# Thirty small marker transfers on SyncE's DMA queue of a decode kernel, behind w3 and behind w4

## The chip, the cores and the metric

The kernel runs on one core of one Trainium2 chip. The metric is the device time of one execution in microseconds, lower is better. A core has TensorE (PE), VectorE (DVE), ScalarE (ACT), GpSimd (POOL) and SyncE (SP). Sixteen DMA engines move data between the chip's memory (HBM) and the core's SBUF; here SP issues nearly all transfers, and ACT two small ones.

## The reference: what is computed

One decode step of a parallel block for 4 sequences, one token each, with D = 576, in bf16:

```python
xn = layernorm(x)                                   # x: 4 x 576
q  = (xn @ wq) as 32 heads of 128                   # wq: 576 x 4096
k, v = the last 2048 of 8192 cached rows            # 4 x 16 kv heads x 2048 x 128, two q heads each
o  = softmax(q k^T / sqrt(128)) v
a  = o @ wo                                         # wo: 4096 x 576
h  = gelu(layernorm(xn) @ w1); hs = shifted(h) @ w2 # 576 x 576 each
x1 = xn + hs
b  = x1 + gelu(layernorm(x1) @ w3) @ w4             # w3: 576 x 4608, w4: 4608 x 576
out = x + a + b
```

The caches dominate: 4 x 16 x 2048 x 128 values of 2 bytes are 33.6 MB for K, and as much for V. With the weights 88.5 MB are read.

## The kernel before

**The stages.** First come the small matmuls with w1, w2, wq and w3, in the order in which these weights land. Then come 16 chunks of K (2 MB each, four ring slots in `kring`): PE transposes each in 8 blocks (line 485), DVE and ACT copy the blocks out of PSUM into `ktb` (469 and 468), and PE multiplies them with q (492). Softmax follows for all heads together. Then come 8 chunks of V (4 MB each, four slots in `vring` and `kring`): DVE spreads the probabilities into padded tiles (545), and PE multiplies (553). Last come h2 @ w4 (36 row blocks) and o @ wo (32 row blocks in five parts of 13, 10, 5, 3 and 1), all added up in one PSUM bank by the helper at line 392, after which DVE and ACT write the halves of the output.

**The order of the work.** The program is collected in one list for each engine. `add` takes a function, the events to wait for, the event that it signals, and a key; line 613 sorts each list by key, and `emit_program` (632) writes the waits and then the instruction. A list is executed in order, so a wait holds all that is behind it on its engine. `add_dma` (192 to 203) puts a transfer into SP's list unless told otherwise; its `dma_start` is line 199, and when the transfer has landed it has added 16 to the semaphore named by its key.

**SP's list around the change.** The keys of w1, w2, wq and w3 are -50, -49, -48 and -47 (lines 269 to 272), and none of them waits. The 16 K chunks have keys 0 to 15 (286 to 288): chunks 0 and 1 wait for nothing, chunks 2 and 3 for q, and each later one for the transposes of the chunk that had its slot. The V chunks have keys KS + 0 to KS + 7, with KS = 132 (289 to 292); the last is cut in two. w4 has key KS + 8 = 140 (273) and waits for a PV step that frees its place; it takes the place of V chunks in `vring`. The five parts of wo have keys 148 to 152 (295 to 299); their waits are for PV steps no later than that of w4. The output is the only other transfer behind them; ACT issues it, as it does x at the start.

**Layouts.** Every transfer on SP's queue has 128 partitions as its outer dimension on the SBUF side. A K chunk is 128 rows of 16 KB, w3 and w4 are 128 rows of 41,472 B, and the last part of wo is 128 rows of 1152 B. The transfers x in and the output have 4 rows of 1152 B.

**POOL's list** holds the memsets and masks of the start, with keys from -100 to below -82, and no waits on DMAs.

Of the kernel before, what the change touches and what calls it, by code (L numbers as in the profile page):

```python
# [6 lines left out]
BF16 = mybir.dt.bfloat16  # L7
# [30 lines left out]
def bass_parallel_sum__sliding_block_cached__mixer_s_mlp__decode_kernel(  # L38
# [24 lines left out]
    NCV, NTV = len(VCH), 2 * NT  # L63
# [6 lines left out]
    with ExitStack() as ctx:  # L70
        def sb(name, shape, dt):
            return ctx.enter_context(nc.sbuf_tensor(name, shape, dt))

        def sem(name):
            return ctx.enter_context(nc.semaphore(name))
# [95 lines left out]
        S = {}  # L171
# [12 lines left out]
        dma_count = {}  # L184
# [3 lines left out]
        def add(engine, emit, waits=(), sig=None, key=0.0, inc=None):  # L188
            seqc[0] += 1
            prog[engine].append(Op(emit, waits, sig, key, seqc[0], inc))  # L190

        def add_dma(pairs, skey, waits=(), key=0.0, engine="sp"):
            if skey not in S:
                S[skey] = sem("s_" + "_".join(str(k) for k in (skey if isinstance(skey, tuple) else (skey,))))
            dma_count[skey] = dma_count.get(skey, 0) + 16 * len(pairs)

            def emit(e):
                for o_, i_ in pairs:
                    e.dma_start(o_, i_).then_inc(S[skey], 16)  # L199
            add(engine, emit, waits, None, key)  # L200
            return ("dma", skey, dma_count[skey])
# [19 lines left out]
        KS = float(NB + 4)  # L221
# [4 lines left out]
        P = lambda *a, **k: add("pool", *a, **k)  # L226
# [52 lines left out]
        def v_src(c, t0, t1):  # L279
# [2 lines left out]
            return A_v_cache[2 * bp:2 * bp + 2, :, k0:k0 + 4 * NTV, :].rearrange(  # L282
                "b h (i t) d -> (b h) i (t d)", t=NTV)[:, :, Dh * t0:Dh * t1]

        t_done = lambda c: f"T{NBLK * c + NBLK - 1}"
        for c in range(NC):
            w = [t_done(c - N_CB)] if c >= N_CB else (["q"] if c >= 2 else [])
# [6 lines left out]
        ev_wo, WOR, a = [], [], 0  # L294
# [176 lines left out]
        for n in range(NB):  # L471
            c, k = n // NBLK, n % NBLK
# [178 lines left out]
        e = nc.tensor  # L651
        emit_program("pe", "pe", e)
        with nc.Fori(0, N_LOOP, engines=[PE]) as it:
# [7 lines left out]
            for j in range(LB):  # L661
                emit_T(e, j, wait)
                if j % NBLK == 2:
                    k = (j // NBLK - 1) % N_CB
# [53 lines left out]
```

## Time and profile before

| what | value |
|---|---|
| median of 2 runs | 214.18 us (213.99 to 214.36) |
| the profiled execution's own time | 213.93 us |
| its span, first to last instruction | 212.6 us |
| mean granted TensorE clock | 0.928 |
| busy: PE, PEld, DVE, ACT, POOL | 172.5, 133.7, 111.9, 58.6, 15.6 us |
| read from HBM | 88.49 MB, 416 GB/s over the span |

A line of a stage or a group names the line of the program, the engine, the operation and "out<-in", with a count behind an x. "Busy" is the time in which an engine executes. The DMA share is the time that the DMA engines' packets took, as a share of 16 engines: 1.0 means that all of them are busy throughout. A packet is one piece that one engine moves. The queues are numbered: q1 is SP's, q10 ACT's, q8 and q14 carry instructions and tables. A row of issues gives the time from an issue to the moment at which the whole transfer has landed, on the last of its engines.

### The profile page before, as it was taken

The page shows a single profiled execution, that of the slowest core. Times are in us where ns is not written, and L with a number is a line of the kernel's source. Part 1 is how long each engine was busy: PE and PEld are TensorE (multiplying, and loading weights), DVE is VectorE, ACT ScalarE, POOL GpSimd, SP SyncE. Part 2 cuts the span into 40 slices and gives each one's busy share as a digit, 9 for nine tenths or more (in the row PEclk, how much of TensorE's full clock was granted, in tenths as well). Part 3 has the DMA queues.
Part 4 walks back from the last instruction along what each step waited for, and adds up shares of the span by engine and source line. Part 5 has one row for each costly group of instructions (what it writes and reads, how often), then busy time and mean ns, then how long its engine had stood idle before and what let it go on. Part 6 is the DMA issues. An engine that isn't in the chain of part 4 may idle for free.

```text
span 212.6 us, 4856 instructions
## 1 busy us (share of the span) xinstructions
PE 172.5 (81%) x2212; PEld 133.7 (63%) x2216; DVE 111.9 (53%) x168; ACT 58.6 (28%) x69; POOL 15.6 (7%) x38
## 2 busy tenths in 40 slices
PE   1456147999999999999996089999989598997495
PEld 0222014888878888887774048988868487883262
DVE  5433200477776777777764869995575444003000
ACT  2004001366665566666656520000000000000000
POOL 8991000000000000000000000000000000000000
PEclk9997855899999999999999589999999889999799
DMA  6999999999999999999999999999999999999993
GB/s 242 453 444 445 429 396 416 432 425 427 429 416 438 432 422 429 435 422 424 432 444 438 444 407 459 413 425 453 407 444 438 419 425 410 451 476 393 407 408 131
DMA packets 5066, 88.65 MB, mean 417 GB/s; under 512 B 568, under 2 KB 704, under 8 KB 1216
## 3 DMA queue, kind: packets, MB, share of 16 engines
q1 hardware_dynamic: 5040, 88.49, 97.7%
q8 instruction: 8, 0.13, 0.3%
q14 instruction: 2, 0.02, 0.0%
q10 hardware_dynamic: 16, 0.01, 0.0%
HBM read 88.49 MB, written 0.00 MB: 416 GB/s over the span
## 4 chain that ended last, share of the span: by engine, by line
DMA 47%; PE 45%; DVE 4%; SPq 1%; ACT 1%; issue 1%
PE ps L485 23%; DMA vring<-in_A_wo_dram 15%; DMA vring<-in_B_w_dram 13%; DMA vring<-in_A_v_cache_dram 12%; PE ps L553 11%; DMA kring<-in_A_k_cache_dram 7%; PE ps L492 6%; PE ps L430 2%; SPq L199 1%; DVE vring L520 1%; DVE rmax L498 1%; DVE ktb L545 1%; PE ps L514 1%; PE ps L347 1%; ACT ktb L468 0%
## 5 line engine op out<-in xcount | busy, mean ns | idle before, releaser
L469 DVE COPY ktb<-ps 128x1024 bf16<-128x1024 bf16 x80 | 53.8, 689 | 23.5 <-PE ps L485 23.4
L485 PEld LDWEIGHTS ps<-perm_bf,kring 128*128 128x128 bf16 x1024 | 58.2, 98 | 8.3 <-issue 7.6
L485 PE MATMUL ps<-perm_bf,kring 128*128 128x128 bf16 x1024 | 61.7, 220 | 0.2
L468 ACT ACTIVATE ktb<-ps 128x1024 bf16<-128x1024 bf16 x48 | 48.0, 1023 | 32.5 <-PE ps L485 32.1
L545 DVE TENSOR_TENSOR ktb<-kring,mH_bf 128x4096 bf16<-128x4096 bf16 x16 | 36.2, 2286 | 14.6 <-PE ps L553 14.6
L553 PE MATMUL ps<-vring,ktb 128*128 128x256 bf16 x256 | 30.3, 282 | 4.3 <-DMA vring<-in_A_v_cache_dram 3.5
L553 PEld LDWEIGHTS ps<-vring,ktb 128*128 128x128 bf16 x256 | 25.7, 101 | 8.5 <-issue 3.6
L553 PE MATMUL ps<-kring,ktb 128*128 128x256 bf16 x256 | 28.6, 273 | 0.9 <-DMA kring<-in_A_v_cache_dram 0.9
L553 PEld LDWEIGHTS ps<-kring,ktb 128*128 128x128 bf16 x256 | 25.0, 98 | 4.5 <-issue 1.1
L608 ACT ACTIVATE out_sb<-ps 4x288 bf16<-4x288 f32 x1 | 0.4, 399 | 84.6 <-PE ps L392 84.6
L492 PE MATMUL ps<-ktb,Qs 128*32 128x512 bf16 x272 | 17.8, 382 | 1.2 <-ACT ktb L468 1.2
L430 PE MATMUL ps<-vring,xs 128*8 128x320 bf16 (+1 forms) x72 | 4.5, 429 | 7.6 <-DMA vring<-in_B_w_dram 7.6
L492 PEld LDWEIGHTS ps<-ktb,Qs 128*32 128x32 bf16 x272 | 5.7, 96 | 6.7 <-DVE ktb L469 1.4
L514 PE MATMUL ps<-vring,pick_bf 128*32 128x256 bf16 x64 | 3.9, 411 | 6.4 <-DVE rinv L532 6.4
L609 DVE CAST out_sb<-ps 4x288 bf16<-4x288 f32 x1 | 0.4, 449 | 15.7 <-PE ps L392 15.7
L392 PE MATMUL ps<-vring,h2T_sb 128*4 128x288 bf16 x72 | 6.2, 347 | 3.1 <-DMA vring<-in_B_w_dram 3.1
L571 DVE TENSOR_SCALAR tmp<-ps,maskd 128x128 f32<-128x128 f32 x2 | 0.7, 350 | 14.8 <-PE ps L553 14.8
L430 PEld LDWEIGHTS ps<-vring,xs 128*8 128x8 bf16 x72 | 2.1, 110 | 9.8 <-DMA vring<-in_B_w_dram 8.0
L330 PE MATMUL ps<-ident_bf,xp_bf 4*128 4x4 bf16 x15 | 0.8, 163 | 8.1 <-DVE xp_bf L314 5.0
L392 PEld LDWEIGHTS ps<-vring,h2T_sb 128*4 128x4 bf16 x72 | 3.7, 101 | 5.8 <-DMA vring<-in_B_w_dram 3.6
L514 PEld LDWEIGHTS ps<-vring,pick_bf 128*32 128x32 bf16 x64 | 2.0, 118 | 8.2 <-DVE rinv L532 6.9
L239 POOL MEMSET ktb<- 128x8192 bf16 x1 | 6.9, 6924 | 0.0
(93 smaller groups left out, 78.6 us busy)
## 6 DMA issues: line engine op xcount, KB each, us to landing
kring<-in_A_k_cache_dram SPq DMA_DIRECT2D x16, 2048.0 KB, 13.8
vring<-in_A_v_cache_dram SPq DMA_DIRECT2D x4, 4096.0 KB, 24.6
kring<-in_A_v_cache_dram SPq DMA_DIRECT2D x3, 4096.0 KB, 34.0
vring<-in_B_w_dram SPq DMA_DIRECT2D x2, 5184.0 KB, 25.1
kring<-in_A_wq_dram SPq DMA_DIRECT2D x1, 4608.0 KB, 15.7
kring<-in_A_v_cache_dram SPq DMA_DIRECT2D x2, 2048.0 KB, 27.4
vring<-in_A_wo_dram SPq DMA_DIRECT2D x1, 1872.0 KB, 26.9
vring<-in_A_wo_dram SPq DMA_DIRECT2D x1, 1440.0 KB, 29.8
```

Of the source, the lines that this page charges most:

```text
L199: e.dma_start(o_, i_).then_inc(S[skey], 16)
L239: P(lambda e: e.memset(ktb[:, NKT // 2 * 1024:NKT * 1024], 0.0), key=-92, inc=(("E", LB - 2), 1))
L347: ins = e.matmul(ps[:, w, :], lhsT=zeros_bf[:, 0:128], rhs=zeros_bf[:, :], start=True, stop=True)
L392: return e.matmul(ACC[h], lhsT=lhsT, rhs=rhs, start=start, stop=stop, tile_position=(0, 32 * h), skip_group_check=True)
L430: ins = e.matmul(H2ps[k][32 * j:32 * j + 2 * B].rearrange("b (p t) -> b p t", t=n), lhsT=x_at(2, s_), rhs=w[:, :, 9 * j + t0:9 * j + t0 + ...
L468: return "act", lambda e: e.activation(out=ktbuf[:, n % NKT], in_=tb[n % 4], func=ACTF.Copy)
L469: return "dve", lambda e: e.tensor_copy(out=ktbuf[:, n % NKT], in_=tb[n % 4])
L485: ins = e.transpose(tb[j % 4][:, t, :], kslot_t(k)[:, 8 * kb + t, :], perm_bf[:])
L492: ins = e.matmul(Sps[32 * u:32 * u + 32, q, :].rearrange("p (t i) -> p t i", t=16), lhsT=Qs[:, k, 32 * u:32 * u + 32], rhs=ktgrp[:, (4 * k ...
L514: ins = e.matmul(ps[32 * j:32 * j + 32, 4 + qt, 256 * ih:256 * (ih + 1)].rearrange("p (t a e) -> p t a e", a=NPAIR, e=2), lhsT=pick_bf[:, ...
L545: return lambda e: e.tensor_tensor(out=PTpad[:, n % 4], in0=PTv[:, qt, NH * h:NH * (h + 1), bp, :].unsqueeze(2).to_broadcast([128, NH, NX, ...
L553: ins = e.matmul(ps[:, 0, 0:256], lhsT=PTpad[:, 2 * (k % 2) + h, 2 * g:2 * g + 2].rearrange("p t h e -> p (t h e)"), rhs=vslot(k)[:, Dh * ...
```

## The change

A new tile, `mark_sb`, of 16 partitions is put behind the others. `marks(n, key)` issues 15 transfers from the top left corner of wo: k rows of 4 + k values, for k from 15 down to 1, so 15 rows of 38 bytes first and one row of 10 bytes last. Each has columns of its own in the tile, and all of a group count on one semaphore. Group 0 has keys of about -45, so it stands between w3 (-47) and K chunk 0 (0). Group 1 has keys just over KS + 8.01, so it stands between w4 (140) and the first part of wo (148). None of the 30 waits for anything. POOL gets two waits, one for each group's full count of 15 x 16 = 240; their key of -1 puts them at the end of its list. Nothing reads `mark_sb`.

```diff
@@ behind v_src, ahead of the loop over the K chunks
+        mark_sb = sb("mark_sb", [16, 2, 256], BF16)
+
+        def marks(n, key):
+            a = 0
+            for k in range(15, 0, -1):
+                add_dma([(mark_sb[0:k, n, a:a + 4 + k], A_wo[0:k, 0:4 + k])], ("mark", n), (), key + 0.001 * (16 - k))
+                a += 4 + k
+        marks(0, -45)
+        marks(1, KS + NCV + 0.01)
+        for n in range(2):
+            P(lambda e, n=n: e.wait_ge(S["mark", n], dma_count["mark", n]), key=-1)
         t_done = lambda c: f"T{NBLK * c + NBLK - 1}"
```

## The prediction, as it was put on record before the result

> **What bounds the kernel now.** I read the page's head and DMA part first, then the chain of waits, then the table of busy time by stage, and last the issues of the DMA queue that the change touches.
>
> ```profile
> span 212.6 us, 4856 instructions
> DMA packets 5066, 88.65 MB, mean 417 GB/s; under 512 B 568, under 2 KB 704, under 8 KB 1216
> q1 hardware_dynamic: 5040, 88.49, 97.7%
> q8 instruction: 8, 0.13, 0.3%
> q10 hardware_dynamic: 16, 0.01, 0.0%
> ```
>
> The reader is to see 97.7%: the packets of SP's queue alone fill all 16 DMA engines for nearly the whole span. The counts also show how a transfer is cut. SP issues 35 transfers of 128 rows, and 35 x (128 + 16) is the 5040 of q1: one packet for each row, and one small one on each of 16 engines that reports the end. The two transfers of 4 rows on ACT's queue, x in and the output, make 16 packets: 4 rows and 4 reports each. The stages (PE, PEld, DVE, ACT, POOL, then granted clock, DMA share, GB/s):
>
> ```profile
> 2.50:29.00 26.50, 9.98 (x84) 4.81 (x84) 10.18 (x34) 3.07 (x7) 13.80 (x31) 0.86 1.01 429
> 92.00:118.00 26.00, 22.83 (x380) 18.27 (x376) 17.56 (x28) 15.61 (x15) 0.00 (x0) 0.99 1.01 433
> 185.00:197.40 12.40, 10.33 (x80) 7.40 (x79) 1.68 (x5) 0.00 (x0) 0.00 (x0) 1.00 1.02 438
> 197.40:208.00 10.60, 8.53 (x112) 5.36 (x114) 0.00 (x0) 0.00 (x0) 0.00 (x0) 0.84 0.95 402
> 208.50:210.40 1.90, 1.26 (x20) 0.53 (x16) 0.00 (x0) 0.00 (x0) 0.00 (x0) 1.00 0.30 116
> ```
>
> The DMA share is 1.0 from 2.5 us to 197.4 us. So the span is the time in which the slowest of 16 engines works through its own list, and a packet put anywhere into that list moves all behind it, to the end. The last row shows that the engines do not end together: in the last 1.9 us only 30% of them work. The end of the chain says what waits for the last engine:
>
> ```profile
> 178.35 31.68 DMA vring<-in_A_wo_dram
> 210.03 0.04 issue
> 210.07 0.70 PE ps L392 x8
> 210.78 0.44 DVE out_sb L609
> ```
>
> The PE chain at the end starts when a wo part has landed; PE is not behind. What delays the slowest engine by 1 us delays the output by 1 us; what delays an engine that is early by up to about 1.9 us costs nothing.
>
> **The change part by part.** It adds 2 x 15 transfers on SP's queue, 30 reports on two new semaphores, a tile of 1 KB a partition behind the others, and two waits on POOL. It removes and reorders nothing else.
>
> *POOL.* Its last instruction of before:
>
> ```profile
> 13.84 2.80 POOL L253 TENSOR_SCALAR_AFFINE_SELECT pick_bf<-pick_bf 128x16 bf16<-128x16 bf16 x16
> ```
>
> The waits come after that row (its list is sorted by key, and -1 is behind all else), nothing is queued behind them, and nobody waits for POOL after 16.6 us. They end when the markers have landed, about 30 us and 200 us. Cost 0; it would cost only if the second group landed behind the output.
>
> *Issue on SP.* The issues that the markers stand between, and the prices of one issue:
>
> ```profile
> 2.17 0.52 SPq L199 DMA_DIRECT2D vring<-in_B_w_dram  x1
> 2.73 1.25 SPq L199 DMA_DIRECT2D kring<-in_A_k_cache_dram  x2
> 20.51 1.18 SPq L199 DMA_DIRECT2D kring<-in_A_k_cache_dram  x2
> 176.55 0.33 SPq L199 DMA_DIRECT2D vring<-in_B_w_dram  x1
> 176.92 2.33 SPq L199 DMA_DIRECT2D vring<-in_A_wo_dram  x5
> 0.81 0.56 ACTq L199 DMA_DIRECT2D x_sb<-in_A_x_dram  x1
> L199 ACTq DMA_DIRECT2D out_dram<-out_sb x1: 279/279/279, 211.3 to 211.3; - x1
> ```
>
> One issue of before takes 0.28 to 0.56 us, the two of 4 rows being both ends; the wo row gives 2.33 / 5 = 0.47 us a piece with its gap. I take 0.47, so a group holds SP for 15 x 0.47 = 7.1 us (bounds 4.2 and 8.4). In the first group that moves the issues of K chunks 0 and 1 from 2.73 to 9.8 us; they end at 11.1 us, before the next issue of 20.51 us, which waits for q and stays. In the second it moves the wo parts from 176.92 to 184.0 us. What hides it is the work that the DMA engines already hold:
>
> ```profile
> vring<-in_B_w_dram SPq DMA_DIRECT2D x1, 5184.0 KB, 27.5
> vring<-in_B_w_dram SPq DMA_DIRECT2D x1, 5184.0 KB, 22.8
> ```
>
> w3 lands at 2.17 + 27.5 = 29.7 us and w4 at 176.55 + 22.8 = 199.35 us, so the engines have transfers until about 29 and, with the first of them at the wo parts, 197.4 us. The cover is gone only where one marker's issue takes over (197.4 - 176.92) / 15 = 1.37 us, more than twice the dearest row. Cost 0; at 2 us each the wo parts would be issued from 206.9 us, and the engines would stand for 9.5 us.
>
> *Packets on the DMA engines.* This is the term that counts. A marker of k rows is k rows and k reports by the count of the 4-row transfers. A group is 15 + 14 + ... + 1 = 120 pairs, both 240 pairs, 480 packets. An engine's share is between 240 / 16 = 15 pairs, if the markers spread evenly, and 30, if each begins on the same first engine. [...]
>
> The price of a pair: the trace of before has no row of 10 to 38 bytes in SP's queue. These are the nearest, in three windows of the DMA view: just ahead of the span (five packets of under 512 B, of kind instruction), about x, and about the output.
>
> ```profile
> DMA packets 5, 0.00 MB, mean 0 GB/s; under 512 B 5, under 2 KB 5, under 8 KB 5
> q14 instruction: 5, 0.00, 0.3%
> q10 hardware_dynamic: 8, 0.00, 10.1%
> DMA packets 8, 0.00 MB, mean 18 GB/s; under 512 B 4, under 2 KB 8, under 8 KB 8
> q10 hardware_dynamic: 8, 0.00, 6.3%
> ```
>
> The first window is 1 us: 0.3% of 16 engine-us is 0.048 us for 5 packets, 10 ns each. The x window is 0.2 us: 10.1% of 3.2 is 0.32 us for 4 rows of 1152 B and 4 reports, 80 ns a pair. The output's is 0.25 us: 6.3% of 4 is 0.25 us, 63 ns a pair. A marker's row is far nearer to the first, so the low end is 2 x 10 = 20 ns a pair, and the high end 80 ns. I take 30 ns, near the low end, with a little for a row that is read and written by itself. The engine with most then works 30 x 0.03 = 0.9 us more (0.6 to 2.4), one with the mean 15 x 0.03 = 0.45 us, and one without any nothing.
>
> *Which of that reaches the end.* An engine ends the program if it is the last. In the last 3.4 us, 207 to 210.4 us, the DMA share by slices of 85 ns falls like this:
>
> ```profile
> DMA  9897988969979696595373663553432100000000
> ```
>
> From about slice 17 (208.5 us) engines run dry one after another, until slice 32 (209.8 us) in packet starts. So engines of all leads between 0 and nearly 2 us exist, and the page does not say whether the late ones are those with many markers. If they have the mean, the end moves by 0.45 us; if the last has none, by 0; if it has all, by 0.9 us. A gain is excluded by the rows: nothing is taken from any engine's list, and an engine that is full at 1.0 in each stage cannot catch up.
>
> **The sum.** The profiled execution took 213.93 us, 1.3 us more than its span of 212.6; the median of the runs shown is 214.18 us (213.99 to 214.36), 0.25 above it. POOL 0, issue 0, packets +0.45: the span becomes 213.05 and the profiled time 214.4 us. On the median it is 214.18 + 0.45 = 214.6 us.
>
> **The rivals.** (1) The late engines hold few markers, so that they fill only the leads of the early ones: the change costs nothing that shows, 214.2 us. For it speaks the ramp above; against it nothing but that the late engines are not named.
>
> [...]
>
> (3) Slower. Tiny transfers that follow each other cannot overlap: on each engine a report holds the queue until its row has landed, and there is no big row behind it to hide that. The price comes from x:
>
> ```profile
> 2.24 0.45 DVE L305 BATCH_NORM_STATS2 stats<-x_sb 4x6 f32<-4x288 bf16 x1 [2.24 <-DMA x_sb<-in_A_x_dram]
> vring<-in_A_wo_dram SPq DMA_DIRECT2D x1, 432.0 KB, 31.7
> vring<-in_A_wo_dram SPq DMA_DIRECT2D x1, 144.0 KB, 31.6
> ```
>
> The x packets lie in the window that ends at 1.9 us, and DVE is released at 2.24 us: 0.34 us from packet to report. At that price the engine with most stands 30 x 0.34 = 10.2 us, less a lead of up to 1.9: 222.5 to 224.4 us, and I name 223.5. It decides (over 2%, 4.3 us) from 4.3 / 30 = 0.14 us a pair where that engine is the last, and from 0.21 us where it has the whole lead. Against it: the last two wo parts are issued 0.47 us apart and land 31.7 and 31.6 us later, so 0.37 us apart, and the 144 KB of the last take 144 x 1024 / 16 bytes at 429 / 16 GB/s = 0.34 us; a report between two transfers leaves no stop of 0.1 us. But there eight rows stand behind each report, and here one.
>
> (4) Issue is much dearer for odd row counts: from 1.37 us a marker the wo parts come late; at 2 us 214.18 + 9.5 = 223.7 us. The rows of 0.28 and 0.56 us speak against it.
>
> **How the numbers follow.** My forecast of 214.6 us has 0.42, rival 1 at 214.2 has 0.26, rival 2 at 215.8 has 0.13, rival 3 has 0.14 and rival 4 has 0.03, which leaves 0.02 for a gain that I can't name. Within 2% of before, 209.9 to 218.5 us, is about what a measurement of this kernel can tell from no change. The first three cases are the same by that: 0.81; slower 0.17; faster 0.02. The range runs from 213.7, a little under the fastest run shown, to 218.0 us, which takes in rival 2's upper end of 217.5, leaves out rivals 3 and 4, and so some 0.19. The likeliest case alone reaches from 214.2 to 216.6 us (0 to 2.4 us added).
>
> **What would show it.** The packets of SP's queue should rise from 5040 to about 5520 and those under 512 B from 568 to about 1048, with its share still at 97% or more. K chunk 0 should be issued near 9.8 us and the first wo part near 184 us, with no stage's DMA share below its row above. The landing of the first K chunks and of the last wo parts should move by the marker time of their slowest engine, under 1 us in the two groups together. The prediction is wrong if the stretch behind w3 (29 to 31 us) or behind w4 shows DMA engines that stand, if one group shifts all later landings by over 2 us, or if a marker's issue takes over 1.37 us.

## The result and the profile after

The changed kernel takes 216.81 us (median of two runs, 216.66 to 216.96) against 214.18. The ratio is 1.0128, with a 95% interval of 1.0112 to 1.0145: 2.6 us slower, under 2%, and a ratio of 1 lies outside the interval. The profiled execution took 216.66 us with a span of 215.3 us, 2.7 us more than before. The page's head, DMA part and chain:

```profile
span 215.3 us, 4887 instructions
DMA packets 5546, 88.66 MB, mean 412 GB/s; under 512 B 1048, under 2 KB 1184, under 8 KB 1696
q1 hardware_dynamic: 5520, 88.50, 97.3%
DMA 67%; PE 23%; DVE 4%; SPq 4%; issue 1%; ACT 1%
```

The counts are those that were worked out: 480 packets more, all under 512 B. The bytes and the queue's share are as before; only the time is longer. The chain that ended last runs through DMA for 67% of the span (47% before): the transfers of K chunks make up 35% of it now, and 7% before, where the chain followed PE's transposes of them. The issues on SP, by start and duration:

```profile
2.80 5.43 SPq L199 DMA_DIRECT2D mark_sb<-in_A_wo_dram  x15
8.27 13.53 SPq L199 DMA_DIRECT2D kring<-in_A_k_cache_dram  x4
178.40 5.39 SPq L199 DMA_DIRECT2D mark_sb<-in_A_wo_dram  x15
183.83 9.90 SPq L199 DMA_DIRECT2D vring<-in_A_wo_dram  x5
```

A group holds SP for 5.4 us, 0.36 us a marker. K chunk 0 is issued at 8.27 us and the wo parts from 183.83 us, both long before a DMA engine is through with the weights ahead of them (the first report of w3 comes at 29.07 us, that of w4 at 197.83 us). So the loss is not there. It is in the stretch behind w3, and again behind w4. Rows by stage, with DMA share and GB/s as the last columns, two of before and then three of after:

```profile
29.00:31.00 2.00, 1.32 (x24) 0.61 (x28) 0.00 (x0) 0.00 (x0) 0.00 (x0) 0.50 0.99 426
31.00:33.00 2.00, 2.00 (x40) 1.09 (x36) 0.00 (x0) 0.44 (x1) 0.00 (x0) 0.50 0.99 426
```

```profile
29.00:31.00 2.00, 1.06 (x20) 0.49 (x24) 0.00 (x0) 0.00 (x0) 0.00 (x0) 0.50 1.07 353
31.00:33.00 2.00, 2.00 (x42) 1.13 (x37) 0.00 (x0) 0.44 (x1) 0.00 (x0) 0.62 0.92 360
33.00:35.00 2.00, 1.51 (x39) 0.96 (x29) 0.00 (x0) 0.38 (x1) 0.00 (x0) 1.00 1.02 426
```

The reader is to see that the share stays near 1.0 while the rate falls from 426 to 353 and 360 GB/s, and is back at 426 in the next two microseconds. Over 4 us that is (852 - 713) x 2 = 278 KB, 17.4 KB an engine, 0.65 us at 26.6 GB/s, as the mean over engines. The engines count as busy because the time is booked on the large packets behind the markers. The trace's packet records show it engine by engine. Engines are told apart here by the smallest marker that they carried; for six of them, behind w4, the durations in ns of the first three packets of wo part 0 (14,976 B, ordinarily 559 ns), the sum over 3 x 559, and that sum with the marker packets' own 12 ns a pair:

```
markers  packet 1  packet 2  packet 3   over    with the pairs
   15      1992       568      1089     1972        2.15 us
   12      1387       565      1126     1401        1.55 us
    9       909       573      1295     1100        1.21 us
    7       565       576      1035      499        0.58 us
    5       571       579       661      134        0.19 us
    0       564       559       569       15        0.02 us
```

The marker packets stand in the records with 7 to 11 ns each and follow each other without a gap. The loss lies behind them: almost nothing for up to five markers, and 0.13 to 0.14 us a pair for 9 to 15. The end of the chain is the one of before, 2.7 us later:

```profile
185.17 27.55 DMA vring<-in_A_wo_dram
212.72 0.04 issue
212.76 0.70 PE ps L403 x8
213.47 0.44 DVE out_sb L620
```

### The profile page after: what moved, and what is told of

Same layout as the page of the kernel before. It is cut to its first block, busy times and chain, and to the rows that moved or that the text cites. A ratio compares the mean times of both kernels' runs of the same rounds, so it can differ in the third digit from the quotient of the medians.

```text
span 215.3 us, 4887 instructions
## 1 busy us (share of the span) xinstructions
PE 171.3 (80%) x2212; PEld 132.2 (61%) x2216; DVE 112.2 (52%) x168; ACT 59.8 (28%) x69; POOL 15.7 (7%) x38
## 2 busy tenths in 40 slices
DMA packets 5546, 88.66 MB, mean 412 GB/s; under 512 B 1048, under 2 KB 1184, under 8 KB 1696
## 3 DMA queue, kind: packets, MB, share of 16 engines
q1 hardware_dynamic: 5520, 88.50, 97.3%
## 4 chain that ended last, share of the span: by engine, by line
DMA 67%; PE 23%; DVE 4%; SPq 4%; issue 1%; ACT 1%
DMA kring<-in_A_k_cache_dram 35%; DMA vring<-in_A_wo_dram 13%; DMA vring<-in_A_v_cache_dram 12%; PE ps L564 11%; DMA kring<-in_A_wq_dram 7%; PE ps L496 7%; SPq L199 4%; PE ps L503 2%; PE ps L380 1%; DVE vring L531 1%; DVE rmax L509 1%; DVE ktb L556 1%; PE ps L525 1%; ACT ktb L479 0%; ACT Qpad L513 0%
## 5 line engine op out<-in xcount | busy, mean ns | idle before, releaser
L496 PEld LDWEIGHTS ps<-perm_bf,kring 128*128 128x128 bf16 x1024 | 57.3, 98 | 10.8 <-issue 8.0
L496 PE MATMUL ps<-perm_bf,kring 128*128 128x128 bf16 x1024 | 62.6, 219 | 1.3 <-DMA kring<-in_A_k_cache_dram 0.4
L479 ACT ACTIVATE ktb<-ps 128x1024 bf16<-128x1024 bf16 x48 | 49.1, 1024 | 32.5 <-PE ps L496 31.7
L403 PE MATMUL ps<-vring,ORT 128*4 128x288 bf16 x64 | 4.6, 286 | 3.3 <-DMA vring<-in_A_wo_dram 3.3
L403 PE MATMUL ps<-vring,h2T_sb 128*4 128x288 bf16 x72 | 4.6, 286 | 3.1 <-DMA vring<-in_B_w_dram 3.1
```

The costliest lines, as they stand in the source:

```text
L403: return e.matmul(ACC[h], lhsT=lhsT, rhs=rhs, start=start, stop=stop, tile_position=(0, 32 * h), skip_group_check=True)
L479: return "act", lambda e: e.activation(out=ktbuf[:, n % NKT], in_=tb[n % 4], func=ACTF.Copy)
L496: ins = e.transpose(tb[j % 4][:, t, :], kslot_t(k)[:, 8 * kb + t, :], perm_bf[:])
```

## The experiments

A report is the small packet at the end of a transfer's part on one engine, a pair is a row and the report behind it, a train is a number of pairs in a row on one engine, and an engine's lead is the time by which it ends before the last one.

The theories are guesses of the author's for the runs to tell apart: (A) a report that follows a tiny row is held until the row has landed, and on its engine holds what is behind it; the engine's reading runs ahead a little, which hides the first few. (B) The tiny row itself is dear. (C) Reports of all engines queue at one semaphore. (D) The issues on SP delay a later transfer. All times over before are the ratio of that comparison times its time of before. The kernels differ in the markers alone. Each diff is cut to the lines that say what is tried and set against the changed kernel; the size of `mark_sb` and POOL's waits follow.

**Which group, which engine.**

```diff
 w3_only                                  w4_only
 marks(0, -45)                           -marks(0, -45)
-marks(1, KS + NCV + 0.01)                marks(1, KS + NCV + 0.01)
```

> Only the group behind w3. Theory A (a report that follows a tiny row holds its engine's write side for about 0.2 us, and the engine can read ahead only some five pairs): the loss is made twice, once behind each group, so one group alone gives about half of the 2.6 us: 215.2 to 215.8 us. Theory B (the row, not the report, is dear): the same here. Theory D (the issue on SyncE delays a later transfer): near 214.2 us here, since the K chunks are covered.

> Only the group behind w4. Theories A and B: the other half, 215.2 to 215.8 us, and the two halves together near the 2.6 us of both groups. Theory D: all 2.6 us, 216.8 us, since the wo parts are those issued late.

Measured: w3_only 215.27 against 213.99 us, ratio 1.0052 (1.0035 to 1.0069), 1.1 us; w4_only 215.38, ratio 1.0061 (1.0045 to 1.0078), 1.3 us. Together 2.4 us, against 2.6 for both groups. Theory D falls: the group behind w3 delays nothing by its issues and costs as much.

```diff
 one_row
-add_dma([(mark_sb[0:k, n, a:a + 4 + k], A_wo[0:k, 0:4 + k])], ...
+add_dma([(mark_sb[0:1, n, a:a + 4 + k], A_wo[0:1, 0:4 + k])], ...
```

> Both groups, but each of the 30 markers has 1 row, so that 30 pairs are left of 240. If the transfers begin on the same first engine (theories A and B), that engine has the same 2 x 15 pairs as with the whole change and loses 2 x 2.2 us less its lead; in the changed kernel it ended with the last ones, so 216.4 to 216.9 us. Theory C (all engines' reports go to one semaphore and queue there, 120 in 2.9 us or 24 ns each): 15 reports in a group cost 0.4 us, so 214.2 to 214.9 us.

Measured: 216.39 us, ratio 1.0114 (1.0098 to 1.0131), 2.4 us over before. An eighth of the pairs costs nearly as much as all of them. Theory C falls, and the 1-row markers do share one engine: when the last part of wo lands, 15 of the 16 reports are there by 210.86 us and one comes at 212.92, where before all came between 208.53 and 210.38. So all these transfers begin on the same engine.

```diff
 all_16 (own_sems: the same with ("mark", n, k) as the semaphore's key, and POOL waits for each)
-for k in range(15, 0, -1):
-    add_dma([(mark_sb[0:k, n, a:a + 4 + k], A_wo[0:k, 0:4 + k])], ("mark", n), (), key + 0.001 * (16 - k))
+for k in range(15):
+    add_dma([(mark_sb[0:16, n, 17 * k:17 * (k + 1)], A_wo[0:16, 0:17])], ("mark", n), (), key + 0.001 * k)
```

> Both groups, 15 markers of 16 rows of 34 bytes each, so that every engine has 15 pairs in each group. Theories A and B: every engine loses 2 x 2.2 us and no lead absorbs it: 218.3 to 218.9 us. Theory C: 240 reports in a group at 24 ns are 5.8 us, twice: above 222 us. The recorded price of 30 ns a pair: 215.1 us.

Measured: 218.8 us, ratio 1.0222 (1.0205 to 1.0239), 4.8 us over before. With every engine loaded alike no lead absorbs anything, and the full price of a group shows: 2.4 us for 15 pairs. Behind w3 the rates are now

```profile
29.00:31.00 2.00, 1.21 (x20) 0.60 (x24) 0.00 (x0) 0.00 (x0) 0.00 (x0) 0.50 1.12 175
31.00:33.00 2.00, 2.00 (x46) 1.19 (x38) 0.00 (x0) 0.44 (x1) 0.00 (x0) 0.66 1.01 303
```

that is (852 - 478) x 2 = 748 KB or 1.76 us an engine, beside the markers' own 0.2 us, all under a share of 1.0 and more.

**Row or report.**

```diff
 one_report: the same 15 rows an engine, in one transfer
+add_dma([(mark_sb[0:16, n, :].rearrange("p (k x) -> p k x", x=17), A_wo[0:16, 0:15 * 38].rearrange("p (k x) -> p k x", x=38)[:, :, 0:17])], ("mark", n), (), key)
```

> Both groups on all 16 engines with the same 15 tiny rows an engine as in all_16, but each group is one transfer, so that an engine has one report in it and not 15. Theory A (the report that follows a tiny row holds the engine): 0 to 0.4 us over the kernel before. [...]

Measured: 214.99 against 213.86 us, ratio 1.0055 (1.0038 to 1.0072), 1.2 us over before. Were the tiny rows dear by themselves (B), the 4.8 us of all_16 would have come again: that is far off. A's 0 to 0.4 us was not met either; it left out that something else costs too: if the rows do, 1.2 / 30 = 0.04 us each. The rest of all_16 goes with its 14 more transfers a group, each with a report on every engine: (4.8 - 1.2) / 28 = 0.13 us each. The rates behind w3 show the small remainder:

```profile
29.00:31.00 2.00, 0.78 (x15) 0.35 (x18) 0.00 (x0) 0.00 (x0) 0.00 (x0) 0.50 1.12 379
31.00:33.00 2.00, 2.00 (x36) 0.98 (x32) 0.00 (x0) 0.16 (x1) 0.00 (x0) 0.50 0.94 401
```

(852 - 780) x 2 = 144 KB are 0.34 us an engine.

```diff
 all_16_w3: all_16 without the group behind w4
-marks(1, KS + NCV + 0.01)
 wide_w3: all_16_w3 with rows of 512 B
-(mark_sb[0:16, n, 17 * k:17 * (k + 1)], A_wo[0:16, 0:17])
+(vring[0:16, 35840 + 256 * k:35840 + 256 * (k + 1)], A_wo[0:16, 0:256])   # w4 waits for them
```

> Only the group behind w3, 15 markers of 16 rows of 34 bytes, to compare the next two with: half of the 4.8 us of all_16 by both theories, 2.2 to 2.6 us over the kernel before.

> Like all_16_w3, with rows of 512 bytes that begin at a multiple of 512 bytes in their tensor. They land in a part of the weights' buffer that is not in use then, and the transfer of w4 waits for them, long after they have landed. Theory A: the reports are the same, so it costs what all_16_w3 costs, plus 15 x 0.02 us for the longer rows at most: 2.2 to 2.9 us over the kernel before. [...]

Measured: all_16_w3 216.41 us, ratio 1.0117 (1.01 to 1.0134), 2.5 us; wide_w3 216.1 us, ratio 1.0118 (1.0088 to 1.0148), 2.5 us; one of its four runs was long, and by the medians it is 2.2. Rows fifteen times as long cost nearly the same. So it is not for the shortness of a 34-byte row that the time was paid: a difference in favour of the wide rows of over 0.8 us, 0.05 us a pair, lies outside these intervals. A smaller one, or one that passes while the engine waits for its reports, is not excluded. No run here tries rows of some KB.

> Like all_16, but each of the 30 markers counts on a semaphore of its own. Theory A1 (a report waits for the tiny row ahead of it to land): no change, 4.5 to 5.0 us over the kernel before. Theory A2 (a report waits for the same engine's last report on the same semaphore): the rows alone are left, as in one_report, 0.9 to 1.5 us over it.

Measured: 218.92 against 214.06 us, ratio 1.0228 (1.0211 to 1.0245), 4.9 us, as all_16. A semaphore shared between reports is not the cause.

**A train, or each by itself.**

```diff
 spread: all_16_w3 with one marker behind each of K chunks 0 to 14
-    add_dma(..., key + 0.001 * k)
-marks(0, -45)
+    add_dma(..., key + k)
+marks(0, 0.5)
```

> The 15 markers of 16 rows of all_16_w3, but one behind each of K chunks 0 to 14 and not 15 in a row. Theory A with reading ahead: a single wait of 0.2 us is covered by what the engine has read ahead, and is won back before the next: 0 to 0.4 us over the kernel before. A fixed price for each pair wherever it stands: 15 x 0.15 = 2.2 us over it, like all_16_w3.

Measured: 214.16 us, ratio 1.0017 (1.0007 to 1.0026), 0.4 us (0.15 to 0.56) against 2.5 for the same 15 markers in a row. Behind w3 the rate does not fall:

```profile
29.00:31.00 2.00, 1.20 (x20) 0.60 (x24) 0.00 (x0) 0.00 (x0) 0.00 (x0) 0.50 1.03 442
31.00:33.00 2.00, 2.00 (x40) 1.01 (x32) 0.00 (x0) 0.44 (x1) 0.00 (x0) 0.50 1.05 451
```

```diff
 all_5, all_30: all_16 with another count
-for k in range(15):
+for k in range(5):        # all_30: range(30)
```

> Like all_16 with 5 markers a group and not 15, again 16 rows of 34 bytes each. Theory A with reading ahead (in the changed kernel the engines with up to 5 markers in a group lost 0.2 us or less there): 0 to 0.5 us over the kernel before. A fixed price for each pair (4.8 us for 30 pairs, 0.16 each): 10 x 0.16 = 1.6 us over it.

> Like all_16 with 30 markers a group. Theory A: each pair beyond the first dozen costs the whole wait of 0.16 to 0.2 us, so 4.8 + 30 x (0.16 to 0.2) = 9.6 to 10.8 us over the kernel before. If only the first pairs of a train were dear, 5 to 6 us over it.

Measured: all_5 214.41 against 214.06 us, ratio 1.0018 (1.0008 to 1.0028), 0.4 us; all_30 225.04, ratio 1.051 (1.0492 to 1.0528), 10.9 us, just over the 10.8 expected. So a group of 5, 15 and 30 pairs costs 0.2, 2.4 and 5.45 us: 0.205 us for each pair from the 15th on, and some 0.7 us of a train hidden (15 x 0.205 - 2.4). In all_30 the wait is long enough to be seen by itself:

```profile
29.00:31.00 2.00, 1.41 (x24) 0.70 (x28) 0.00 (x0) 0.00 (x0) 0.00 (x0) 0.50 2.69 138
31.00:33.00 2.00, 2.00 (x40) 1.05 (x36) 0.00 (x0) 0.44 (x1) 0.00 (x0) 0.51 0.00 0
33.00:35.00 2.00, 1.52 (x42) 1.08 (x30) 0.00 (x0) 0.38 (x1) 0.00 (x0) 1.00 0.89 246
```

A packet is counted where it begins. At 138 GB/s some 17 packets of 16 KB, about one an engine, begin between 29 and 31 us and then none for 2 us; those few have the whole wait in their durations, 3.8 to 4.7 us each where 0.61 is usual, which gives the impossible share of 2.69.

**The reports themselves.** The traces also keep the time of every count on a semaphore, and there the wait is seen directly. In one_row a single engine carries all markers. Its 15 pairs behind w3 begin within 0.18 us, from 29.18 to 29.36 us, but their reports arrive at 29.73, 29.92, 30.10 and so on to 32.33 us, 0.18 to 0.19 us apart. The three packets of K behind them take 1.82, 0.63 and 1.18 us, where 0.61 is usual, and the third ends at 32.97 us. So the engine begins each packet in time and what is slow is the end: the reports come out one by one, the three packets behind them take 1.80 us more than usual together, and the third ends 0.64 us after the last report. In the changed kernel too the last three reports behind w3 arrive 0.18 us apart, at 31.98, 32.16 and 32.35 us. In own_sems, where each marker has a semaphore of its own, the median report of a marker follows that of the marker before by 0.16 to 0.21 us. Behind w3 the reports of wide_w3 arrive over 3.6 us and those of all_16_w3 over 3.8, so longer rows do not slow them.

## Why the prediction was right and where it was not

The time of 216.81 us lies in the range of 213.7 to 218.0, and "within 2%" was the likeliest case. The forecast of 214.6 us was 2.2 us short: 0.45 us added where 2.6 were measured. That the range held was in part luck: its own likeliest case ended at 216.6 us, and it reached to 218.0 for the sake of rival 2, which did not bring the time there.

- *POOL, and the issue on SP at 0: right.* The issue was estimated at 7.1 us a group and took 5.4. w3_only and w4_only cost alike, though what the first group's issues delay, K chunks 0 and 1, do not start before the engines get through with w3, at about 29 us (their first packet begins at 28.89 us).
- *The count of packets and the uneven load: right.* 5520 and 1048 came out as written, and one_row shows one engine with 15 pairs in each group.
- *Which engine ends last: right in kind.* In the table behind w4 an engine with 9 markers and the one with 15 reach the end of packet 3 within 0.02 us of each other. This also fits the single groups, with leads that are assumed and were not measured one by one. The 9-marker engine, taken as one with no lead, loses 1.2 us in each, which is the 1.1 and 1.3 us of w3_only and w4_only and 2.4 for both. The 15-marker engine loses 2 x 2.15 = 4.3 us, less the lead of up to 1.9 us that the ramp showed: 2.4, as in one_row. The forecast had taken an engine with the mean, 15 pairs in both groups, where this one has 18.
- *The price of a pair: the step that failed.* The prediction took 30 ns, from the duration of small packets in the records, with bounds of 20 and 80 ns. The rows alone do cost about that (one_report: 40 ns at most). But the wait of the reports is not in any packet's duration in the trace of before. It makes a pair 0.134 us at 9 in a row, 0.143 at 15 and 0.205 for each further one, outside the upper bound. 2 x 9 x 0.134 = 2.4 us is the sum with the right price.
- *The bounds of that price were too narrow.* The upper one was taken from pairs that stand alone and not in a train. The row that spoke for the wait, 0.34 us from x's packets to its report, was used for rival 3 alone and belonged in the bounds.
- *Rival 3 had the right kind of loss at too high a price.* It gave 0.34 us for each of 30 pairs, 10.2 us. The wait is 0.205 us (all_30), the first 0.7 us of each train is hidden, and one engine's lead takes the rest, so the time stayed under rival 3's threshold. Its own doubt was the right one: between the wo parts eight rows stand behind each report, and there nothing shows; between markers one row does.
- *Rival 2, a dearer small row, falls* as the cause of the 2.6 us, as far as the intervals reach: rows of 512 B cost as much as rows of 34 B (wide_w3 and all_16_w3, 2.5 us each). No run shows the dearer small row from which its 215.8 us and its upper end of 217.5 us were worked out; what the runs showed is 0.04 us a row at most (one_report), and what that is made of stays open. Rivals 1 and 4 fall with the 2.6 us and with the issue of 0.36 us.
- *What would show it.* "Under 1 us in the two groups together" was wrong. "DMA engines that stand" was right as a sign and wrong as to where to look: the share does not show it, GB/s does.

That the reports of an engine come out one by one, about 0.2 us apart, is seen in the records (0.18 to 0.19 us in one_row, 0.16 to 0.21 in own_sems); what each waits for was not shown. With the same rows the time goes with the number of reports in a row (4.8 us in all_16, 1.2 in one_report), and neither with the row's size (2.5 us at 34 B and at 512 B) nor with the semaphore (4.9 us in own_sems). But in every train here a row stands ahead of each report, and each report is also the end of a transfer. So no run tells a wait for the row ahead from a least distance between two reports of one engine, or from a price at the end of each transfer. What they do show is the price, 0.205 us for each pair from the 15th of a train on (all_30 against all_16), and that the packets behind the train pay it (3.8 to 4.7 us each in all_30, where 0.61 is usual).

## What to carry to other kernels

Where the DMA engines bound a kernel, count reports in a row on one engine, not packets or bytes: here a tiny transfer among large ones cost about 0.03 us (spread: 0.4 us for 15), but each one from the fifteenth of a train on cost its engine 0.2 us (all_30: 10.9 us against 4.8 in all_16), and delayed what stood behind it. Pack small loads into one transfer with many rows (one_report: 1.2 us against 4.8), or put them between large ones (spread: 0.4 against 2.5). The transfers of one row all loaded the same engine here (one_row: one report in 16 came 2.06 us behind the others), so look at what that engine loses, less its lead, and not at the mean.

## What the runs showed of the hardware that was not expected

A DMA share of 1.0 does not mean full rate: it was 1.07 at 353 GB/s in the changed kernel, and 2.69 and then 0.00 in all_30, because a packet that waits counts as busy from its start (3.8 to 4.7 us each in all_30). Read it beside GB/s.

An issue can also take long. In the changed kernel the last wo part's issue begins at

```profile
185.64 8.09 SPq L199 DMA_DIRECT2D vring<-in_A_wo_dram  x1
```

and takes 8.09 us, where the five parts of before took 2.33 us together. It ended at 193.7 us, before w4 had landed (first report at 197.83 us), so it cost nothing; what SP waits for there was not tried.
